# A decode step bound by its loads: 128 rows of two weight matrices moved to half of the partitions, one K tile asked for before the FFN weights, and a shorter list of transfers at the end

## Chip, cores, metric

One core of one Trainium2 chip. The metric is the device time of one execution in microseconds (us), median of several. A program on one core has shown no slower state in this study. Runs of one group share a chip and their runs of the kernel before; the groups fell on chips 2, 4 and 10 of the pool.

## The reference

A sum of three terms over the layer-normed input: attention of one query per head over a cache of 8192 keys, a SwiGLU FFN, and the input itself.

```python
# x (4, 1, 512); k_cache, v_cache (4, 32, 8192, 128); wq (512, 4096); wo (4096, 512)
# w_gate, w_up (512, 1792); w_down (1792, 512); all bfloat16
xn = layernorm(x)
q = (xn @ wq).reshape(4, 1, 32, 128).transpose(0, 2, 1, 3)
p = softmax(einsum("bhqd,bhkd->bhqk", q, k_cache) * 128 ** -0.5)
o = einsum("bhqk,bhkd->bhqd", p, v_cache)
attn = o.transpose(0, 2, 1, 3).reshape(4, 1, 4096) @ wo
ffn = (silu(xn @ w_gate) * (xn @ w_up)) @ w_down
out = x + attn + ffn
```

The two caches are 537 MB of the 551 MB that the core has to read.

## The kernel before

The 128 pairs of batch and head are 32 tiles of four heads. A tile has 8 MB of K and 8 MB of V, each loaded by one transfer to 128 partitions, 64 KB of consecutive bytes per partition. Three slots of 64 KB per partition take turns. VectorE transposes K in place, TensorE makes the scores and later the products with V. All loads are issued by SyncE in program order; each waits until its slot is free.

The parts that the change touches:

```python
def load_ffn():
    t_ = slot()
    w, w3 = EC * F, 2 * EC * F + FC * D               # EC = 4 rows of 512 per partition
    nc.sync.dma_start(out=t_[:, 0:w], in_=B_w_gate.rearrange("(p c) f -> p (c f)", c=EC))
    nc.sync.dma_start(out=t_[:, w:2 * w], in_=B_w_up.rearrange("(p c) f -> p (c f)", c=EC))
    nc.sync.dma_start(out=t_[:, 2 * w:w3], in_=B_w_down.rearrange("(p c) e -> p (c e)", c=FC))
# wq is loaded in the same way; partition p has rows 4p to 4p + 3, and the transposed
# input xnt_w[:, c] has the elements c, c + 4, c + 8, ...
...
for i in range(NT - 1):                               # one K/V tile per turn
    turn_k(i, ...)
    if i >= 3:
        pv_to(i - 2, NK)                              # rest of the product with V tile i - 2
        load_k(i + 1)
    for g in range(NTG):
        score(i, g)
    if i == 0:
        load_ffn()
    elif i == 1:
        load_k(2)
    else:
        load_v(i)                                     # the last but one in two pieces
    ...                                               # softmax, first half of V tile i - 1
    if i == 1:
        load_v(1)
        do_ffn()
        load_k(3)
# the last tile: V in small pieces, wo in between and behind
load_wo(0, NB4 - 2)
v_from(n, t_, H * D, 0, (T // 4, T // 4))
...
v_from(n, t_, 0, T // 2, (48, 32, 24, 16, 8))
load_wo(NB4 - 2, NB4 - 1)
load_wo_heads(H - 4, H - 2)
load_wo_heads(H - 2, H - 1)
load_wo_heads(H - 1, H)
```

## Time and profile before

| | before |
|---|---|
| time, median | 1284.72 us (1284.67 to 1284.85) |
| span of the profile | 1282.9 us |
| read from memory | 550.77 MB |
| busy: TensorE, VectorE, ScalarE | 79%, 57%, 2% |
| DMA share from 60 to 1200 us | 1.00 |
| DMA share from 1270 to 1279.4 us | 0.64 |

How to read it: an engine at 79% could only set the time in a stretch of its own; what is at 1.00 for 1140 us is the set of sixteen DMA engines. One row of the table of stretches has the stretch, its length, busy time and instructions of TensorE, of its weight loads, of VectorE, ScalarE and GpSimd, then TensorE's granted clock, the DMA share (16 engines busy = 1.00) and GB/s. In a stretch of a few us, packets that begin inside it are counted whole, so that the share can come out a little above 1. The lines themselves stand in the prediction below.

### The profile page before, as it was taken

To read this page: it belongs to the slowest core of one execution; us is meant where nothing else is said; L and a number is where in the kernel's file an instruction comes from. 1 tells how busy PE (TensorE), PEld (TensorE's weight loads), DVE (VectorE), ACT (ScalarE), POOL (GpSimd) and SP (SyncE) were. 2 spreads that over 40 slices of the span, in tenths; PEclk is the share of its full clock that TensorE was granted. 3 is DMA by queue.
4 is the path that set the end of the run, shared out by engine and by line. 5 is a ranking of instruction groups with operands and counts; after the bars stand their busy time and mean duration, and the time that the engine had idled before them with its cause. 6 is when DMAs were issued, how large, how long until landed. Compare 5 with 4: busy or idle time off the path is not lost.

```text
span 1282.9 us, 11312 instructions
## 1 busy us (share of the span) xinstructions
PE 1012.6 (79%) x5170; PEld 464.0 (36%) x5170; DVE 736.6 (57%) x621; ACT 30.1 (2%) x71; POOL 5.9 (0%) x12
## 2 busy tenths in 40 slices
PE   1697777977778977778877879877779787789786
PEld 0254333433334433333333334333334333334346
DVE  4856644665545665554656545666445756446651
ACT  1000000000000000000000000000000000000000
POOL 1000000000000000000000000000000000000000
PEclk9897889988899988889888899888898888899886
DMA  9999999999999999999999999999999999999997
GB/s 423 426 432 428 436 437 432 432 437 430 434 432 440 428 432 437 440 426 426 446 432 430 438 436 423 439 436 432 430 438 434 434 430 432 443 428 432 435 416 327
DMA packets 12359, 551.49 MB, mean 430 GB/s; under 512 B 1292, under 2 KB 1816, under 8 KB 3096
## 3 DMA queue, kind: packets, MB, share of 16 engines
q1 hardware_dynamic: 12304, 550.78, 99.3%
q8 instruction: 40, 0.66, 0.2%
q14 instruction: 7, 0.06, 0.0%
q10 hardware_dynamic: 8, 0.00, 0.0%
HBM read 550.77 MB, written 0.00 MB: 429 GB/s over the span
## 4 chain that ended last, share of the span: by engine, by line
DMA 54%; PE 37%; DVE 8%; issue 0%; ACT 0%; SPq 0%; DVEq 0%
DMA slot<-in_A_k_cache_dram 50%; PE sps L74 19%; PE oacc L74 17%; DVE slot L303 8%; DMA slot<-in_A_wo_dram 4%; PE mps L74 0%; PE mps L322 0%; DVE ptz L340 0%; PE yo_ps L74 0%; ACT p__324 L331 0%; DVE mx L316 0%; SPq L96 0%; SPq L98 0%; ACT res L497 0%; SPq L99 0%
## 5 line engine op out<-in xcount | busy, mean ns | idle before, releaser
L303 DVE STREAM_TRANSPOSE slot<-slot 128x2048 uint32<-128x2048 uint32 (+1 forms) x198 | 561.8, 2901 | 283.1 <-DMA slot<-in_A_k_cache_dram 283.0
L74 PE MATMUL sps<-slot,zq 128*128 128x512 bf16 x2048 | 524.5, 420 | 234.2 <-DVE slot L303 234.2
L74 PE MATMUL oacc<-slot,ptz 128*16 128x512 bf16 x1920 | 430.8, 380 | 0.0
L74 PEld LDWEIGHTS <-zq 128*128 128x128 bf16 x2048 | 213.2, 104 | 542.2 <-issue 237.2
L74 PEld LDWEIGHTS <-ptz 128*16 128x16 bf16 x1920 | 195.3, 106 | 208.7 <-issue 12.7
L316 DVE TENSOR_REDUCE mx<-sps 128x1 f32<-128x512 f32 x32 | 22.1, 692 | 105.0 <-PE sps L74 105.0
L74 PEld LDWEIGHTS <-slot 128*128 128x128 bf16 (+2 forms) x716 | 25.7, 111 | 26.3 <-issue 14.0
L350 DVE RECIPROCAL rcp<-mps 128x4 f32<-128x4 f32 x32 | 5.8, 183 | 43.3 <-PE mps L74 43.2
L325 DVE TENSOR_REDUCE nm<-mps 128x4 f32<-128x64 f32 x32 | 7.2, 224 | 35.8 <-PE mps L322 35.8
L74 PE MATMUL xps<-ptz,slot 128*128 128x4 bf16 x512 | 15.3, 169 | 6.2 <-DMA slot<-in_A_v_cache_dram 6.2
L74 PE MATMUL yo_ps<-slot 128*4 128x128 bf16 (+1 forms) x60 | 3.5, 309 | 15.3 <-DMA slot<-in_A_x_dram 13.7
L74 PEld LDWEIGHTS mps<-rowb,rs 128*128 128x128 f32 x64 | 9.7, 191 | 14.4 <-issue 12.7
L74 PE MATMUL mps<-rowb,rs 128*128 128x4 f32 x64 | 12.5, 266 | 1.5 <-ACT p__324 L331 1.5
L74 PE MATMUL xps<-rowy,o 128*32 128x4 f32 (+1 forms) x226 | 10.7, 205 | 2.2 <-DVE o L375 2.2
L293 DVE COPY zq<-qt 32x8 bf16<-32x8 bf16 x64 | 11.1, 174 | 0.7
L322 PE MATMUL mps<-ident_f,mx 128*128 128x128 f32 x32 | 10.5, 327 | 0.8 <-DVE mx L316 0.8
L74 PEld LDWEIGHTS xps<-rowy,o 128*32 128x32 f32 (+1 forms) x226 | 10.0, 155 | 2.8 <-DVE o L375 2.8
L322 PEld LDWEIGHTS mps<-ident_f,mx 128*128 128x128 f32 x32 | 4.3, 134 | 13.8 <-issue 6.3
L395 DVE TENSOR_TENSOR otn<-xps,rcp 32x16 bf16<-32x16 f32 x28 | 4.8, 171 | 6.6 <-PE xps L74 4.5
L74 PE MATMUL yo_ps<-slot,otn 128*4 128x128 bf16 x128 | 7.2, 310 | 1.3 <-DMA slot<-in_A_wo_dram 1.3
L385 DVE TENSOR_TENSOR otn<-xps,rcp 128x16 bf16<-128x16 f32 x1 | 0.2, 174 | 12.8 <-PE xps L74 12.8
L74 PEld LDWEIGHTS <-otn 128*4 128x4 bf16 x128 | 6.7, 123 | 1.6 <-issue 1.5
(146 smaller groups left out, 187.0 us busy)
## 6 DMA issues: line engine op xcount, KB each, us to landing
slot<-in_A_v_cache_dram SPq DMA_DIRECT2D x2, 4096.0 KB, 32.3
slot<-in_A_wq_dram SPq DMA_DIRECT2D x1, 4096.0 KB, 12.4
slot<-in_A_v_cache_dram SPq DMA_DIRECT2D x2, 2048.0 KB, 36.9
slot<-in_A_wo_dram SPq DMA_DIRECT2D x1, 3072.0 KB, 30.3
slot<-in_B_w_gate_dram SPq DMA_DIRECT2D x1, 1792.0 KB, 24.1
slot<-in_B_w_up_dram SPq DMA_DIRECT2D x1, 1792.0 KB, 27.9
slot<-in_B_w_down_dram SPq DMA_DIRECT2D x1, 1792.0 KB, 31.8
slot<-in_A_v_cache_dram SPq DMA_DIRECT2D x1, 1536.0 KB
```

The source lines that it names most:

```text
L74: nc.tensor.matmul(out_ap, lhsT=lhsT, rhs=rhs, start=start, stop=True, skip_group_check=True, **kw)
L293: nc.vector.tensor_copy(out=zq[a * QB:(a + 1) * QB, :, :, XO + a * QB].rearrange("p b (j r) -> p r j b", r=2), in_=qt[a * QB:(a + 1) * QB, ...
L303: nc.vector.transpose(out=ap, in_=ap)
L316: nc.vector.reduce_max(out=mx[:], in_=s_ps[n][:], axis=AX.X)
L322: nc.tensor.matmul(mps[:, 0:P], lhsT=nmx.pop(n)[:, 0:1].to_broadcast([P, P]), rhs=ident_f[:, :], is_transpose=True, start=True, stop=True, ...
L325: nc.vector.tensor_reduce(out=nm[:], in_=by_row(mps[:, 0:P]), axis=AX.X, op=ALU.max, negate=True)
L350: nc.vector.reciprocal(out=rcp[j][:, :, b], in_=mps[:, P:P + HT])
L385: nc.vector.tensor_tensor(out=otn[:, j * HT:(j + 1) * HT, :], in0=xps[:], in1=rcp.pop(j)[:], op=ALU.mult)
L395: nc.vector.tensor_tensor(out=otn[q0:q1, j * 4:j * 4 + 4, :], in0=xps[q0:q1], in1=r_[q0:q1, y, :].unsqueeze(1).to_broadcast([QB, 4, B]), o ...
```

## The change

Its intent is to balance the sixteen DMA engines. 384 rows of wq and of w_gate stay on 128 partitions (three each); the other 128 rows go to partitions 0 to 63, two each, by two transfers whose source view has 8 as outermost dimension. Since a row of the weight is then on another partition, the transposed input gets five more chunks. The third K tile is asked for ahead of the FFN weights, and the end has four transfers fewer.

```diff
+    C0, C1 = 3, 2
+    NC = C0 + C1
+    R0 = C0 * P
+    def load_split(t_, base, w, n):
+        nc.sync.dma_start(out=t_[:, base:base + C0 * n], in_=w[0:R0, :].rearrange("(p c) n -> p (c n)", c=C0))
+        src = w[R0:D, :].rearrange("(s b a c) n -> s a b (c n)", s=2, b=4, a=8, c=C1)
+        for s in range(2):
+            nc.sync.dma_start(out=t_[s * QB:(s + 1) * QB, base + C0 * n:base + NC * n], in_=src[s])
...
-    nc.sync.dma_start(out=wq_t[:, 0:EC * H * Dh], in_=A_wq.rearrange("(p c) n -> p (c n)", c=EC))
+    load_split(wq_t, 0, A_wq, H * Dh)
...
+        load_split(t_, 0, B_w_gate, F)
...
         if i == 0:
+            load_k(2)
+        elif i == 1:
             load_ffn()
-        elif i == 1:
-            load_k(2)
+        elif i == 2:
+            load_k(3)
...
+        if i == 2:
+            row_sums(i)
+            do_ffn()
+            load_v(2)
...
-    v_from(n, t_, H * D, 0, (T // 4, T // 4))
+    v_from(n, t_, H * D, 0, (T // 2,))
...
-    v_from(n, t_, 0, T // 2, (48, 32, 24, 16, 8))
+    v_from(n, t_, 0, T // 2, (64, 40, 24))
...
-    load_wo_heads(H - 2, H - 1)
-    load_wo_heads(H - 1, H)
+    load_wo_heads(H - 2, H)
```

(Cut: the five chunks of the transposed input, the loops over chunks in the q and gate matmuls, and small changes of order that go with the new sequence.)

## The prediction

> **What bounds the kernel now.** I read the page first: how busy the engines are, then the DMA rows of the slices and the queues.
>
> ```profile
> span 1282.9 us, 11312 instructions
> ...
> DMA  9999999999999999999999999999999999999997
> GB/s 423 426 432 428 436 437 432 432 437 430 434 432 440 428 432 437 440 426 426 446 432 430 438 436 423 439 436 432 430 438 434 434 430 432 443 428 432 435 416 327
> DMA packets 12359, 551.49 MB, mean 430 GB/s; under 512 B 1292, under 2 KB 1816, under 8 KB 3096
> ...
> q1 hardware_dynamic: 12304, 550.78, 99.3%
> q8 instruction: 40, 0.66, 0.2%
> q14 instruction: 7, 0.06, 0.0%
> ```
>
> The sixteen DMA engines are busy in every slice but the last. TensorE is at 79% and VectorE at 57%, so neither sets the time: 550.78 MB have to be read, and 434 GB/s is the rate. The chain of waits names DMA (54%) and gives the rest to work that only releases buffers for later transfers. The one slice under 9 is the last, so I asked for busy time by stretch, where the last two columns are DMA share and GB/s, and for the chain's end.
>
> ```profile
> 60.00:1200.00 1140.00, 922.27 (x4200) 413.43 (x4200) 661.97 (x545) 22.77 (x59) 0.00 (x0) 0.89 1.00 434
> ...
> 1260.00:1270.00 10.00, 6.60 (x182) 6.20 (x178) 2.98 (x5) 0.00 (x0) 0.00 (x0) 0.67 0.99 418
> 1270.00:1279.40 9.40, 5.78 (x152) 5.38 (x154) 0.17 (x1) 0.00 (x0) 0.00 (x0) 0.50 0.64 248
> ```
>
> ```profile
> 1257.44 20.81 DMA slot<-in_A_wo_dram
> 1278.24 0.04 issue
> 1278.29 1.90 PE yo_ps L74 x32
> ```
>
> For 1140 us the DMA share is 1.00. In the last 9.4 us it is 0.64: over a third of the engines have run dry while the rest still work. The program ends with the last wo transfers and 1.9 us of matmuls behind them.
>
> Why do they run dry? The trace's packet records (start, duration, size) can be strung into sixteen chains, since each packet starts within some 20 ns of the end of the one before it on its engine. A 64 KB packet takes 2.42 us on every chain. Eight chains are broken by the 16 KB packets of queue q8 (instruction fetches), five times each: a gap of 0.86 to 0.95 us and a neighbour lengthened by some 0.5, together 1.4 us. The completion writes of successive loads show the sum: the sixteen engines end K tile 1 within 1.5 us, the last tile before the tail within 7.55 us. At that point seven engines lie at 0 to 0.70 us, eight at 5.7 to 7.55 (7.1 to 7.55 once each has five fetches), and one, which I call L, at 4.44. L has none of q8, but five of the seven 8 KB packets of q14, at 0.83 us each, spaced as 8 KB of VectorE's instructions would be. The last loads land at 1279.34 on the late eight; the light seven are done near 1271.8 to 1272.5, L near 1279.34 - (7.55 - 4.44) = 1276.2.
>
> **What the Trainium skill says.** "Runtime: NRT & Kernel Launch", Instruction fetch mechanics: instruction memory is refilled by DMA in 16 KiB blocks of 256 instructions, the cost "mostly hidden". The q8 packets are 16 KB, and TensorE's 9770 rows at 64 bytes are 38 blocks, near the 40 seen; but the cost is not hidden here, because it is taken from engines that are the bound. "DMA: Bandwidth & Descriptors", Why a DMA increments its semaphore by 16 and not by 1: a DMA runs on the largest k up to 16 that divides the slowest dimension of both sides, on the lowest-numbered k engines. The trace agrees in what it shows: the 3-row and the 1-row load of x make four packets on three chains, two of them on one chain, which must be engine 0. These three chains (engines 0 to 2) have no q8 packet. So q8 very likely lives on engines 8 to 15, and L is among 3 to 7. The same page, Rules for kernel authors, advises against two transfers to disjoint partition halves because both use the same engines; here the halves are used to choose the engines.
>
> **The change part by part.**
> 1. *128 rows of wq and w_gate.* Their source view has 8 as outermost dimension, so k = 8: engines 0 to 7 alone. From the durations (65536 B every 2414 ns, 14336 every 531.5, 4096 every 156) a packet costs 5.4 ns + 36.76 ns per KB of 1000 bytes. wq per engine: before, 8 of 32 KB, 9.68 us. After, engines 8 to 15 have 8 of 24576 B, 7.27 us (-2.41), and engines 0 to 7 another 8 of 16384 B, 12.14 us (+2.46). w_gate likewise: 4.26 us becomes 3.20 (-1.05) and 5.37 (+1.11). Sum: the late eight lose 3.46 us, the other eight gain 3.57. The difference, 7.0 us, is just the lag of the q8 engines.
> 2. *Order of K tile 2 and the FFN.* No byte more or less. The queue has to stay ahead of the engines, and these lines of the timeline show where it is nearly caught:
>
> ```profile
> 52.21 0.33 SPq L241 DMA_DIRECT2D slot<-in_B_w_gate_dram  x1
> ...
> 77.59 0.33 SPq L107 DMA_DIRECT2D slot<-in_A_k_cache_dram  x1
> ...
> 91.89 0.33 SPq L120 DMA_DIRECT2D slot<-in_A_v_cache_dram  x1
> ```
>
> The FFN's transfers end at 82.9 on the first engine; K tile 2 is asked for at 77.6, 5.3 us ahead. With part 1, x and K tile 0 land some 2.5 us later, so the asking moves to about 80, while engines 8 to 15 would be done at 79.4: they would starve for 1 to 2 us. In the new order K tile 2 is asked for near 54.7 (V tile 0 ends on them at 67.7), the FFN near 80 (87.0), V tile 1 near 94.4 (98.7). So this part protects part 1 and is worth nothing by itself.
> 3. *Fewer transfers at the end.* Bytes are the same. One piece of V of 16 KB rows and two of the small pieces fewer save 24 packets of 5.4 ns per engine, and four completions of 6 ns: 0.15 us. The last transfer is two heads of wo: 8 matmuls at 59 ns follow it (1.88 us/32), not 4: +0.2.
> 4. *More small work.* Eight more q matmuls (3.60/32 = 0.11 us each, 0.9 us), 14 more gate matmuls (6.83/112 = 61 ns, 0.85 us), five transposes and four copies: on engines with 20% and more to spare, beside DMA.
>
> **The sum.** End of transfers: late eight 1279.34 - 3.46 - 0.15 = 1275.7; light seven 1272.5 + 3.57 - 0.15 = 1275.9. But L: 1276.2 + 3.57 - 0.15 = 1279.65. The last semaphore needs all sixteen, so **one engine keeps the gain**: the last landing moves by +0.3, the matmuls behind it by +0.2 at most, of which little shows as they are already queued. 1284.72 + 0.3 = 1285.0. I shade it to 1284.9 for the rival below.
>
> **The rivals.**
> - *Balance pays in full.* If L's fetches are not on an engine that gains rows, or are hit less, all end near 1275.8: 3.4 us gained, about 1281.4. For it: the sizes fit the lag so well that somebody measured it. Against: L has no q8 packet, and the eight that have one leave only engines 0 to 7. About one in four.
> - *All sixteen engines share the 128 rows* (the view is lowered otherwise). No shift: 1284.5 from the tail alone. Little speaks for it, as the program after compilation has a 32-partition target in two transfers.
> - *Wrong half, or starvation early.* Were q8 on the engines that gain, the end would be 3.6 us later, 1288.3; a gap in the queue near 80 to 100 us on half the engines would add 1 to 2 us. Against it the x packets and the margins of part 2.
>
> **Range and chances.** The centre is 1284.9. Downwards the range must hold most of the full balance, upwards some error of L's position: 1281.4 to 1286.0. No rival moves the time by 2% (25.7 us), since the transfers bind throughout: same 0.99.
>
> **What would show each step.** Part 1: the spread of completion writes should be some 7 us from the FFN on with engines 8 to 15 first, and shrink to nothing but L at the end. In the stretches, the DMA share of the last 8 us falls from 1 to near 1/16 over its last 4 us if L is alone; if the full balance holds, it stays over 0.9 until the end and the last landing is near 1276. Part 2: no gap of DMA share between 3 and 110 us. Part 3: no wait of the queue on V landings in the tail (12.3 us in three before). The prediction is wrong if VectorE's fetches lie on engines 8 to 15, or if a transfer to half the partitions runs at another rate than 2.42 us per 64 KB.

## The result

1288.31 us (1288.03 to 1288.82, four runs) against 1284.70 us: 3.6 us slower. The ratio is 1.0029, with an interval of 1.0011 to 1.0046; ratios here are the mean time of one kernel's fast runs over that of the other's of the same rounds, so not quite the ratio of the medians. By 2% the two are the same, as predicted; the time is outside the range, which ended at 1286.0.

The page of the changed kernel, the lines that answer to those of before:

```profile
span 1286.3 us, 11373 instructions
...
DMA  9999999999999999999999999999999999999996
GB/s 420 427 418 451 425 435 433 432 431 438 431 433 437 433 431 437 436 431 435 432 429 445 429 425 443 433 428 437 435 435 433 431 439 431 431 439 433 434 420 283
DMA packets 12071, 551.49 MB, mean 429 GB/s; under 512 B 1260, under 2 KB 1784, under 8 KB 2872
...
q8 instruction: 40, 0.66, 0.2%
q14 instruction: 7, 0.06, 0.0%
```

The bytes are the same, the rate is the same until the last slice, and the last slice has 283 GB/s where it had 327. All of the loss shows at the end. The stretches of the changed kernel, same columns as before, cut finer there:

```profile
60.00:1200.00 1140.00, 916.09 (x4209) 412.79 (x4209) 661.70 (x545) 22.77 (x59) 0.00 (x0) 0.89 1.00 434
1270.00:1275.00 5.00, 3.58 (x128) 3.49 (x128) 0.00 (x0) 0.00 (x0) 0.00 (x0) 0.50 0.88 361
1275.00:1277.00 2.00, 1.50 (x50) 1.44 (x51) 0.00 (x0) 0.00 (x0) 0.00 (x0) 0.50 0.43 156
1277.00:1279.50 2.50, 1.93 (x53) 1.84 (x52) 0.00 (x0) 0.00 (x0) 0.00 (x0) 0.50 0.22 80
1279.50:1282.50 3.00, 2.02 (x54) 1.92 (x52) 0.17 (x1) 0.00 (x0) 0.00 (x0) 0.50 0.13 48
```

0.88 is 14 engines (two have run dry before 1270), 0.22 some three to four, and 0.13 is two. So the balance did come: most engines end near 1275.9. But **two engines work on alone until 1282.5**. Before, the eight late engines ended together, from 1278.9 to 1279.3. The chain of waits ends as before, only 3.2 us later:

```profile
1256.34 25.15 DMA slot<-in_A_wo_dram
1281.48 0.04 issue
1281.53 1.97 PE yo_ps L78 x32
```

The queue kept ahead, as worked out for part 2. These are the issues of K tile 2, the FFN and V tile 1 in the changed kernel (start, duration, engine, line):

```profile
54.24 0.33 SPq L122 DMA_DIRECT2D slot<-in_A_k_cache_dram  x1
79.62 0.33 SPq L101 DMA_DIRECT2D slot<-in_B_w_gate_dram  x1
...
93.92 0.33 SPq L135 DMA_DIRECT2D slot<-in_A_v_cache_dram  x1
```

Part 3 did what it should, too. Among the waits of the load queue, the kernel before has this line from 1200 us on (waited in all, times, longest); the changed kernel has no wait of the kind.

```profile
SPq L281 <- DMA slot<-in_A_v_cache_dram: 12.3, 3, 4.5
```

### The profile page after: what moved, and what is told of

Its sections match the earlier page's. It is cut to its first block, busy times and chain, and to the rows that moved or that the text cites. A ratio compares the mean times of both kernels' runs of the same rounds, so it can differ in the third digit from the quotient of the medians.

```text
span 1286.3 us, 11373 instructions
## 1 busy us (share of the span) xinstructions
PE 1007.8 (78%) x5197; PEld 463.1 (36%) x5197; DVE 737.2 (57%) x625; ACT 30.1 (2%) x71; POOL 6.0 (0%) x12
## 4 chain that ended last, share of the span: by engine, by line
DMA 55%; PE 34%; DVE 9%; issue 0%; ACT 0%; SPq 0%; DVEq 0%; ACTq 0%
DMA slot<-in_A_k_cache_dram 45%; PE sps L78 18%; PE oacc L78 14%; DMA slot<-in_A_v_cache_dram 8%; DVE slot L334 7%; DMA slot<-in_A_wo_dram 2%; DVE ptz L371 1%; PE mps L78 1%; PE xps L78 1%; PE yo_ps L78 0%; PE mps L353 0%; DVE oacc L404 0%; DVE o L406 0%; SPq L104 0%; DVE mx L347 0%
## 5 line engine op out<-in xcount | busy, mean ns | idle before, releaser
L78 PE MATMUL sps<-slot,zq 128*128 128x512 bf16 x2048 | 515.8, 415 | 230.6 <-DVE slot L334 230.4
L78 PEld LDWEIGHTS <-zq 128*128 128x128 bf16 x2048 | 210.6, 103 | 532.3 <-issue 222.9
L78 PEld LDWEIGHTS <-slot 128*128 128x128 bf16 (+3 forms) x730 | 28.4, 110 | 32.3 <-issue 18.7
L78 PE MATMUL mps<-xnt_w,slot 128*128 128x4 bf16 (+1 forms) x126 | 10.2, 203 | 2.7 <-DVE rcp L381 2.7
L353 PE MATMUL mps<-ident_f,mx 128*128 128x128 f32 x32 | 10.3, 322 | 1.6 <-DVE mx L347 1.6
```

What stands on the lines that cost most here:

```text
L78: nc.tensor.matmul(out_ap, lhsT=lhsT, rhs=rhs, start=start, stop=True, skip_group_check=True, **kw)
L353: nc.tensor.matmul(mps[:, 0:P], lhsT=nmx.pop(n)[:, 0:1].to_broadcast([P, P]), rhs=ident_f[:, :], is_transpose=True, start=True, stop=True, ...
```

## The experiments

Theory F (for fetches): two of the eight engines that carry the instruction fetches of q8 are among engines 0 to 7. They keep their lag of some 7 us and are given 3.57 us of rows on top. The rivals: the new order or the new end costs the time (T); the split costs a fixed amount, whatever its size; the fetches do not set the end at all.

### Which engine is which: markers

To the kernel before (and, in a second run, to the changed one) fifteen tiny loads are added, one per tile, of n rows for n = 1 to 15. By the rule that the prediction cites, each runs on engines 0 to n - 1. The trace agrees in what it shows: the marker of n rows is on n chains, and they are again among the chains of the next marker.

```diff
+    def mark(n):
+        r, w = n % 2 * 32, 4 * n
+        nc.sync.dma_start(out=pad_t[r:r + n, 0:w], in_=A_wq[0:n, 0:w])
...
             load_v(i)
+            if 3 <= i <= 17:
+                mark(i - 2)
```

> The kernel before, with fifteen marker loads added (n rows of 8n bytes each, n = 1 to 15, one per tile), so that engine e of 0 to 15 carries just the markers with n > e and every chain of packets gets its number. Theory F (fetches): two of the eight engines that serve the 16 KB fetches of q8 have numbers below 8, six above; the engine with five 8 KB fetches of q14 is below 8 too. The prediction's assumption: all eight are 8 to 15. Time within 0.5 us of before.

Correct, 1284.71 us in one run. In the packet records a packet starts 3 or 4 ns before the one before it on its engine ends (some 15 ns around a fetch), and after eight packets of 64 KB comes a completion write. Strung by these two signs, all sixteen chains up to 1240 us get a number (engines 1 and 15 near 450 us, and 4 and 13 near 600 us, come within 1 ns of each other and are told apart by their markers):

```
markers carried    engine   fetch packets on the chain, us
n = 1 to 15        0        none
n = 2 to 15        1        q14 (8 KB): 755
n = 3 to 15        2        none
n = 4 to 15        3        q14 (8 KB): 60, 333, 568, 846, 1069
n = 5 to 15        4        q14 (8 KB): 557
n = 6 to 15        5        q8 (16 KB): 158, 442, 721, 1020
n = 7 to 15        6        q8 (16 KB): 194, 478, 760, 1049
n = 8 to 15        7        none
n = 9 to 15        8        none
n = 10 to 15       9        q8 (16 KB): 233, 517, 796, 1087
n = 11 to 15       10       q8 (16 KB): 257, 553, 832, 1126
n = 12 to 15       11       q8 (16 KB): 41, 292, 583, 875, 1161
n = 13 to 15       12       q8 (16 KB): 82, 331, 622, 906, 1188
n = 14 and 15      13       q8 (16 KB): 100, 370, 661, 945, 1222
n = 15             14       q8 (16 KB): 119, 408, 699, 981
no marker          15       none
```

The fetches are **not** on engines 8 to 15: they go round 5, 6 and 9 to 14, one after another, and 8 and 15 have none. L, the engine of most of the 8 KB fetches, is 3, among 3 to 7 as predicted.

> The changed kernel with the same markers. Theory F: the two chains that end last, near 1282.5, have numbers below 8 and carry q8 fetches; two chains above 8 have none and end first, some 10 us earlier. The prediction's assumption: the last chain is one without q8. Time within 0.5 us of the changed kernel, 1288.3.

Correct, 1288.42 us in one run. Many chains of this run cross within a few ns, so that it names fewer engines by itself; the chain of the 8 KB fetches again has the markers from n = 4 on, engine 3. The moved rows of w_gate, packets of 7168 bytes, are on eight chains, those of engines 0 to 7. As in the untouched changed kernel, two engines are left at the end (DMA share 0.13 from 1279.5 to 1282 us), and the last loads end at 1282.99. For those two the untouched changed kernel is clearer: the two chains that end last fall back at 723, 756, 1014 and 1035 us, just where q8 packets of 16 KB stand, and both have packets of 7168 bytes. The completion writes of the untouched changed kernel show all groups at once: the sixteen of one load near 1207 us come as two at 1201.3 and 1201.7 (as engines 8 and 15 would, relieved and free of q8), eleven from 1205.8 to 1207.8, one at 1211.3 (as L would) and two at 1212.8 and 1212.9 (as 5 and 6 would).

### Undo the split, or do it alone

The changed kernel with both weights on all 128 partitions again:

```diff
-    load_split(wq_t, 0, A_wq, H * Dh)
+    nc.sync.dma_start(out=wq_t[:, 0:EC * H * Dh], in_=A_wq.rearrange("(p c) n -> p (c n)", c=EC))
-        load_split(t_, 0, B_w_gate, F)
+        nc.sync.dma_start(out=t_[:, 0:w], in_=B_w_gate.rearrange("(p c) f -> p (c f)", c=EC))
```

(and the four-chunk loops of before with it)

> The changed kernel with wq and w_gate loaded over all 128 partitions again; the new order of K tile 2 and FFN, and the shorter list of transfers at the end, stay. Theory F: the 3.6 us come from the split alone, so 1284.5 (1284.7 less 0.15 for the packets saved). Rival T (order or tail cost it): 1287 to 1288.5.

Measured: 1284.56 us (1284.49 to 1284.80), ratio 0.9999 to before. The 3.6 us are gone; order and end together are worth the 0.15 us of packets saved, if anything, which is below what the interval resolves.

The kernel before with the split alone, old order and old end:

> The kernel before with the split of wq and w_gate alone; old order and old end. Theory F: 1284.7 + 3.57 = 1288.3; engines 8 to 15 may starve for 1 to 2 us at the FFN, but they have slack, so nothing more. Rival T: 1284.7 to 1285.5.

Measured: 1288.28 us (1287.97 to 1288.30), ratio 1.0027. The split alone is the whole loss. The packet records show the gap in the queue that the new order was for: between 80 and 81 us only 10.3 of the 16 engines were busy, between 81 and 82 12.4, and all again from 83. It cost nothing here, as the engines that starved had time to spare at the end. So the new order guards against something real that does not bind in this kernel.

### Half doses

wq alone split, and w_gate alone split (each otherwise the changed kernel):

```diff
 # wq_only
-        load_split(t_, 0, B_w_gate, F)
+        nc.sync.dma_start(out=t_[:, 0:w1], in_=B_w_gate.rearrange("(p c) f -> p (c f)", c=EC))
 # gate_only
-    load_split(wq_t, 0, A_wq, H * Dh)
+    nc.sync.dma_start(out=wq_t[:, 0:EC * H * Dh], in_=A_wq.rearrange("(p c) n -> p (c n)", c=EC))
```

> The changed kernel with only wq split; w_gate over all partitions again. Theory F (two fetch engines below 8 also get the moved rows): end set by them, 1284.56 + 2.46 = 1287.0. If the split cost a fixed amount, or the FFN part did it: 1284.6 or 1288.3.

> The changed kernel with only w_gate split; wq over all partitions. Theory F: 1284.56 + 1.11 = 1285.7. If wq alone did it: 1284.6; a fixed cost: 1288.3.

Measured: 1287.11 us (1287.00 to 1287.23) and 1285.53 us (1285.48 to 1285.57). The loss follows the rows given to engines 0 to 7, term by term:

| kernel | moved rows add to engines 0 to 7 | 1284.56 + that | measured |
|---|---|---|---|
| no split | 0 | 1284.56 | 1284.56 |
| w_gate alone | 1.11 us | 1285.67 | 1285.53 |
| wq alone | 2.46 us | 1287.02 | 1287.11 |
| both (the changed kernel) | 3.57 us | 1288.13 | 1288.31 |

A fixed cost of a split transfer would not scale so. A lower rate to half of the partitions would, but the packet records exclude it: packets of 16384 bytes took 611 ns (median) in the kernel before and with the split alike.

### Eight fetches more

If fetches make the late engines late, more TensorE instructions must cost time although TensorE is not the bound. To the kernel before, 1024 matmuls of 4 columns are added, without use:

```diff
+        if 3 <= i < 29:
+            for _ in range(40 if i < 23 else 37 if i < 27 else 38):
+                mm(rs_t[i][1][0:4, 256:260], zq[:, 0, 0, 0:4], zq[:, 0, 0, 0:4], start=True)
         row_sums(i)
```

> The kernel before with 1024 tiny matmuls (2048 TensorE instructions, results unused) spread over 26 tiles: TensorE has room for their 60 us. 2048 instructions of 64 bytes are 8 more fetches of 16 KB, one for each of the eight engines. Theory F: q8 shows 48 packets, the end is 1.4 us later, 1286.1. Rival (fetches do not set the end, TensorE work is hidden): 1284.7.

Measured: 1286.26 us (1285.98 to 1286.41) against 1284.77: 1.49 us more, ratio 1.0011 (interval 0.9996 to 1.0026, so that the size is known better from the medians and the trace than from the ratio). TensorE's busy time rises by 7.4 us only, from 1012.6 to 1020.0, spread over 26 tiles. The last big packet ends at 1281.05 instead of 1279.34. The page of this kernel counts the fetches:

```profile
q8 instruction: 48, 0.79, 0.2%
```

The same late stretch in this kernel, then in the kernel before: at 1279.4 to 1281 the loads of before are over, here they still run on six engines' worth.

```profile
1279.40:1281.00 1.60, 1.01 (x20) 1.01 (x21) 0.00 (x0) 0.00 (x0) 0.00 (x0) 0.50 0.38 127
```

```profile
1279.40:1281.00 1.60, 0.77 (x16) 0.48 (x10) 0.28 (x1) 0.26 (x1) 0.00 (x0) 0.50 0.00 0
```

### Give the rows to engines that carry no fetches

With the numbers known, engines 0 to 2 are the ones to fill. A first try, without any new layout, splits one V tile by partitions (on top of the kernel without the split):

```diff
+        if n == 6:
+            c = (T - 144) * Dh
+            nc.sync.dma_start(out=t_[:, 0:c], in_=src[:, 0:c])
+            p0 = 0
+            for k in (112, 3, 3, 3, 3, 4):
+                nc.sync.dma_start(out=t_[p0:p0 + k, c:], in_=src[p0:p0 + k, c:])
+                p0 += k
+            return
```

> The kernel without the split (order and end as changed), and V tile 6 loaded so that its last 144 of 256 columns go as 112 partitions over all engines and 16 partitions as four times 3 and once 4: engines 0 to 2 get four packets of 36864 bytes more, engine 3 the same as ever, the other twelve one less (1.36 us). Theory F: engines 0 to 2 have 7 us to spare, all fetch engines lose 1.36 us: 1284.56 - 1.36 = 1283.2, faster than both kernels. If engines 0 to 2 carried fetches: 1284.6 + 5.4 = 1290; if the engine does not matter: 1284.6.

Measured: 1305.63 us (1304.59 to 1307.57, four runs), ratio 1.0164: a miss, in the wrong direction and far too large. The packets of 36864 bytes took 2.74 us on average instead of 1.36, while those of 28672 bytes of the same tile kept their 1.06 (median). To see which transfers were slow, the 16 partitions were loaded by one transfer on all sixteen engines; no engine is favoured then:

```diff
+            for p0, p1 in ((0, 112), (112, P)):
+                nc.sync.dma_start(out=t_[p0:p1, c:], in_=src[p0:p1, c:])
```

> As the kernel without the split, but the last 144 columns of V tile 6 in two transfers, 112 partitions and 16. Both run on all sixteen engines, 7 packets and 1, the same bytes for each: no engine is favoured. If the slow packets of the run with threes (36864 bytes in 2.65 us instead of 1.36) come from a transfer to 112 partitions, where an engine's partitions are not a multiple of 8: packets again over 2 us and 1290 to 1300. If they came from the transfers to 3 and 4 partitions: 1284.6.

Measured: 1302.27 us in one run; the packets of 36864 bytes again took 2.97 us on average. This page row shows the dip where tile 6 is loaded (the tenth and eleventh of 40 slices):

```profile
GB/s 419 420 427 447 426 440 431 434 436 284 357 434 431 436 432 436 432 434 436 426 442 425 444 422 442 425 438 428 440 432 436 434 430 438 428 440 428 438 417 316
```

The packet records tell the two transfers apart in time. Until 320 us only packets of the transfer to 112 partitions start, seven for each engine, and the 102 of them take 1.95 to 2.83 us: it runs at about half rate by itself. The last 26, with the sixteen of the small transfer among them, take up to 5.57 us, so the small transfer is not cleared: while it ran, packets were slower still. Why is open. The first try says nothing about theory F.

The second try uses the layout trick of the change itself on w_gate: 96 of its 128 moved rows go to engines 0 to 2, 32 to engines 0 to 3, each engine writing the partitions that it writes in the changed kernel.

```diff
+        s3 = B_w_gate[384:480].rearrange("(s b a c) f -> s a b (c f)", s=2, b=4, a=3, c=4)
+        s4 = B_w_gate[480:512].rearrange("(s b a) f -> s a b f", s=2, b=4, a=4)
+        for s in range(2):
+            nc.sync.dma_start(out=t_[s * QB:s * QB + 12, 3 * F:7 * F], in_=s3[s])
+            nc.sync.dma_start(out=t_[s * QB:s * QB + 16, 7 * F:8 * F], in_=s4[s])
```

> The kernel without the split of wq (order and end as changed); of the 128 moved rows of w_gate, 96 go to 12 partitions in two transfers (slowest dimension 3: engines 0 to 2) and 32 to 16 partitions in two (slowest dimension 4: engines 0 to 3); eight gate chunks instead of four. Engines 0 to 2 get 8 packets of 14336 bytes and 8 of 3584 more, engine 3 8 of 3584; all lose 1.05 us of w_gate: net +4.3, 0 and -1.05. Theory F (fetches on 5, 6 and six above 7): the late eight lose 1.05 us and the others have room, 1284.56 - 1.05 = 1283.5, faster than both kernels. If engines 0 to 2 have no room: 1284.6 to 1287.8.

Measured: 1284.44 us (1284.17 to 1285.57, five runs) against 1284.68 for before, ratio 1.000 (interval 0.9987 to 1.0014). By its time this is a miss, as 1283.5 was expected. The transfers did what was expected. The last stretch, in this kernel and then in the kernel without the split:

```profile
1278.00:1279.40 1.40, 1.20 (x21) 1.04 (x20) 0.00 (x0) 0.00 (x0) 0.00 (x0) 0.50 0.01 3
```

```profile
1278.00:1279.40 1.40, 1.08 (x22) 1.07 (x23) 0.11 (x1) 0.00 (x0) 0.00 (x0) 0.50 0.38 133
```

The last big packet ends at 1278.09 here and at 1279.36 there: 1.27 us earlier, where 1.05 was expected. The time fell by 0.1 to 0.2 us only, less than these runs resolve. Part of the way between shows in the timeline: the matmuls behind the last loads, which ran without a break in the kernel without the split (x32, 2.00 us), are broken here.

```profile
1277.12 0.80 PE L74 MATMUL yo_ps<-slot,otn 128*4 128x128 bf16 x11 [0.47 <-DMA slot<-in_A_wo_dram]
1278.20 1.33 PE L74 MATMUL yo_ps<-slot,otn 128*4 128x128 bf16 x21 [0.28 <-issue]
```

The pause of 0.28 us has no releaser that the profile shows; a q8 packet from 1276.0 to 1276.9 us suggests that TensorE waited for its own instructions, but no run tests that. The cast of the result starts at 1279.47 instead of 1280.26, and the output's last completion write ends at 1280.82 instead of 1281.61, both 0.79 us earlier. The span of the profile is 0.5 us shorter (1282.4 against 1282.9). Over all runs the spans have a median of 1282.2 against 1282.9 before, while the time outside the span is 2.0 to 3.4 us here and 1.7 to 1.9 before. So part of the gain is lost outside of what the profile covers, and why stays open. This version is 3.9 us below the changed kernel and level with the kernel before.

## Why the prediction was wrong, point by point

- **What bounds the kernel, and why engines run dry at the end: right.** The eight more fetches of q8 moved the end by 1.49 us where 1.4 us per fetch was read from the gaps.
- **Where the fetches live: this step failed.** The prediction put it so: "So q8 very likely lives on engines 8 to 15, and L is among 3 to 7." The observation beneath it holds, engines 0 to 2 carry no q8 packet. The conclusion took three engines for eight. The markers show fetches on 5, 6 and 9 to 14, and none on 8 and 15, so that 5 and 6 got 3.57 us of rows on top of their lag and ended at 1282.50. Knowing that eight of sixteen engines are late says nothing on which eight; the split addresses engines by number, so the numbers were the thing to settle.
- **Part 1, sizes: right.** Of the eight engines that carry fetches, two (5 and 6) got +3.57 us instead of -3.46. For 5 and 6 the same sum is 1278.9 to 1279.34 (their end before), + 3.57 - 0.15, so 1282.3 to 1282.8; the trace has 1282.50. With half doses it holds within 0.2 us.
- **"One engine keeps the gain": right in kind, wrong in who.** L was worked out to end at 1279.65; the stretch to 1279.5 still has three to four engines, the one after it two. Had the fetches been on none of 0 to 7, L would by the prediction's sum have left the time at 1285; no run tests that. Engines 5 and 6 were behind it.
- **One reading was off, without effect.** The prediction has 9770 TensorE instructions, 38 blocks. The page has 5170 matmuls and 5170 weight loads, 10340 in all; at 64 bytes that is 40.4 blocks, which fits the 40 fetches better.
- **Parts 2 and 3: right.** Issues at 54.2, 79.6 and 93.9 us against 54.7, 80 and 94.4; no gap; the waits on V pieces are gone; 1284.56 without the split. The starvation foreseen for the old order is seen in the run with the split alone.
- **The rivals: the one that came true was named, with its figure, and then put aside.** "Were q8 on the engines that gain, the end would be 3.6 us later, 1288.3"; it was 1288.31. That it fits to 0.01 us is luck, as the last landing in the profile moved by 3.16 us. What spoke against it, "the x packets", was the three engines again. One carrier among the gainers is enough for it, since the last engine sets the end, so its chance was much larger than that of a wrong half as a whole. The range should have reached 1288.5.

## What to carry to other kernels

When loads bind, the slowest of the sixteen DMA engines sets the end, and instruction fetches are load too: string packets into chains and see who is late. Before moving bytes between engines, number the engines with marker transfers of 1 to 15 rows, since one misplaced engine undoes the balance of all others. And a split transfer need not keep the full rate: here transfers to 32, 12 and 16 partitions on 8, 3 and 4 engines kept it, one to 112 partitions on all sixteen ran at about half of it. Measure the duration of its packets before building on it.

## What the Trainium skill lacked or had wrong

- "Runtime: NRT & Kernel Launch", Instruction fetch mechanics, has the cost of crossing a block as "mostly hidden". In a kernel bound by loads it is not: each 16 KB fetch takes some 1.4 us of one DMA engine, and eight more of them cost 1.49 us of kernel time. The page does not say which DMA engines serve the fetches; here TensorE's go round 5, 6 and 9 to 14, one after another.
- The same section gives blocks of 16 KiB. TensorE's are; the other instruction packets of the run are 8 KB (queue q14, seven in the kernel before), five of them on engine 3 at 0.83 us each.
- "DMA: Bandwidth & Descriptors", Why a DMA increments its semaphore by 16 and not by 1: the rule for the number of engines agrees with these runs (the moved rows of w_gate came in packets of 7168 bytes on just eight chains). No page gives the rate of a transfer to 112 partitions, seven for each of sixteen engines: its packets of 36864 bytes took 2.6 us in the median, where 1.36 us is the estimate from the other packets.
